# Gated linear recurrence and cos-gated layer: one masked score product per head and chunk in place of seven block sizes, with the gates' product divided out of the keys

## Chip, cores and metric

The kernel runs on one core of one Trainium2 chip, in float32. The metric is the device time in microseconds of one execution. The median of three runs of the kernel before is 1408.85 us (1404.82 to 1410.23).

## What is computed

Two stages. The first is a linear recurrence with complex gates; the second is a gated layer on its output. Cut to what matters:

```
mag = sqrt(a_re**2 + a_im**2)                       # B=4, H=8, S=768, D=48
a   = (a_re + i a_im) * minimum(mag, 0.999) / (mag + 1e-6)
for t in range(S):                                  # S is a complex 48x48 state per (b, h)
    S = a[t][:, None] * S + outer(k[t], v[t])
    y[t] = einsum('d,de->e', q[t], real(S))
x = y as (3072, 384)
h = x @ w_in                                        # 384 x 2048
out = (h * cos(h)) @ w_out                          # 2048 x 384
```

The gates lie near 0.9: a_re is 0.85 to 0.95 and a_im is normal with deviation 0.1. The weights come as float64, and the kernel turns their bits into float32 on the chip.

## The kernel before

Time is cut into chunks of 128 steps, six per batch entry and 24 in all. Two chunks make a group, so there are 12 groups. Work goes in iterations: iteration `it` does `gates(it)`, `chunks(it-1)` and `layer(it-2)`, three stages of a pipeline over groups, and `weave` mixes their pieces by a position between 0 and 1. There are 14 iterations. The scheduler of the language then orders each engine's instructions.

**Gates** (`g_log` L201 to `g_stack` L280, tiles of 128 x 768 for a group): magnitude and tangent of each gate by Ln and Exp on ScalarE with a correction step on VectorE and GpSimd; the angle by Arctan; running sums of the angles over the chunk by a product with a triangular matrix (`phs`, L263, and L266 for what the chunk before left); cos and sin; and the stacked keys `ks` and queries `qs` (L293), 96 wide, cos part and sin part.

**Chunks**: `mT`, `kT` and `qT` (magnitudes, keys, queries) are transposed per head through TensorE (L304, copied out of PSUM by ScalarE, L306). For a pair s < t in a chunk the product of magnitudes between them is needed. It is never divided out: seven block sizes (1, 2, ... 64) each take one matrix product per head (`lv`, L330, 128 x 64), a masked copy into the score tile `atm` on VectorE (L333), and then, for the next block size, half of `qT` times a total on VectorE and half of `kT` times a total on GpSimd (both L341). So one level waits for the scaling of the level before, and two chunks run alternately. Then `yp` (L354 scores times values, L357 queries times state), the diagonal term on GpSimd and VectorE (L348, L360), the new state (`kp`, L371, transposes the scaled keys back; `sp`, L375), and `xp` (L395), which transposes the result for the layer.

**Layer**: `mm1` (L403, `hp`, eight pieces of 128 x 512), the cosine in five steps on ScalarE and VectorE (L409 to L416), `mm2` (L422, `op`, 16 products of 128 x 384 per chunk), a copy and the store. The weights are loaded and converted (`from_double`, L136 to L164, six VectorE steps and one GpSimd add on each of 14 parts) at the end of iteration 0.

TensorE runs its instructions in order; a product in float32 that is not a transpose shows in the trace as two records, so 1344 `lv` products are 2688 records.

Of the kernel before, what the change touches and what calls it, by code (L numbers as in the profile page):

```python
# [11 lines left out]
F32 = mybir.dt.float32  # L12
U8 = mybir.dt.uint8
U32 = mybir.dt.uint32
I64 = mybir.dt.int64
# [10 lines left out]
ROUND = 12582912.0  # L26


@with_exitstack
def kernel(  # L30
    ctx: ExitStack,
    tc: tile.TileContext,
    q: bass.AP,
# [29 lines left out]
    NJ = DF // C  # L63
# [3 lines left out]
    consts = ctx.enter_context(tc.tile_pool(name="consts", bufs=1))  # L67
    wts = ctx.enter_context(tc.tile_pool(name="wts", bufs=1))
    ld = ctx.enter_context(tc.tile_pool(name="ld", bufs=2))
    gt = ctx.enter_context(tc.tile_pool(name="gt", bufs=1))  # L70
    ft = ctx.enter_context(tc.tile_pool(name="ft", bufs=2))
    pa = ctx.enter_context(tc.tile_pool(name="pa", bufs=5, space=PSUM))
    pm = ctx.enter_context(tc.tile_pool(name="pm", bufs=3, space=PSUM))

    step_np = np.arange(C)
    mask_np = np.zeros((C, LV, C // 2), np.uint8)
    for l in range(LV):
        m = 1 << l
        right = step_np[(step_np // m) % 2 == 1]
        mask_np[:, l] = ((step_np[:, None] // (2 * m) == right[None, :] // (2 * m))  # L80
                         & ((step_np[:, None] // m) % 2 == 0))
    sums_np = (step_np[:, None] <= step_np[None, :]).astype(np.float32)
    last_np = np.zeros((C, C), np.float32)
    last_np[C - 1] = 1.0

    def constant(array, dtype, name):
        t = consts.tile(list(array.shape), dtype, name=name)
        nc.scalar.dma_start(out=t, in_=nc.inline_tensor(array, name=name + "_const").ap())
        return t

    def scalar_tile(value, name):
# [4 lines left out]
    X = [dict() for _ in range(NG)]  # L96
    Y = [dict() for _ in range(N)]
# [13 lines left out]
    sums = constant(sums_np, F32, "sums")  # L111
    ident = constant(np.eye(C, dtype=np.float32), F32, "ident")
# [20 lines left out]
                    from_double(stage, dst, src)  # L133

    def from_double(stage, dst, src):
        """dst = the doubles of which src has the bits, to the nearest float32 (0 below 2^-126).  # L136

        A double's exponent field is 11 bits wide, a float's 8: what falls between the top bit
        and the low seven only tells the range.
        """  # L140
        shape = list(dst.shape)
        raw = stage.tile(shape, I64, tag="raw", name="raw")
        nc.sync.dma_start(out=raw, in_=src)
# [335 lines left out]
            msb = ctx.enter_context(tc.tile_pool(name="msb", bufs=2))  # L479


# [1 line left out]
_INS = ['q', 'k', 'v', 'a_re', 'a_im', 'moe_w_in', 'moe_w_out']  # L483
_OUTS = [((3072, 384), 'float32')]
# [25 lines left out]
```

## Time and profile before

| | |
|---|---|
| profiled execution, own span | 1405.6 us |
| median of three runs | 1408.85 us |
| TensorE busy (matmul) | 1181.8 us, 84% |
| VectorE / GpSimd / ScalarE busy | 801.7 / 653.1 / 446.2 us |
| mean granted TensorE clock | 0.843 |

The profiled execution's span is 3.25 us below the median of the runs. A page's 40 slices of some 35 us each show the busy share in tenths; PEclk is the share of its full clock that TensorE was granted. A row of a timeline gives the start and the length in us; the length of a row of matmuls overlaps with the next row's start, since they are pipelined, so the pace of a row is read from start to next start.

### The profile page before, as it was taken

The page shows a single profiled execution, that of the slowest core. Times are in us where ns is not written, and L with a number is a line of the kernel's source. Part 1 is how long each engine was busy: PE and PEld are TensorE (multiplying, and loading weights), DVE is VectorE, ACT ScalarE, POOL GpSimd, SP SyncE. Part 2 cuts the span into 40 slices and gives each one's busy share as a digit, 9 for nine tenths or more (in the row PEclk, how much of TensorE's full clock was granted, in tenths as well). Part 3 has the DMA queues.
Part 4 walks back from the last instruction along what each step waited for, and adds up shares of the span by engine and source line. Part 5 has one row for each costly group of instructions (what it writes and reads, how often), then busy time and mean ns, then how long its engine had stood idle before and what let it go on. Part 6 is the DMA issues. An engine that isn't in the chain of part 4 may idle for free. (4 is left out here: it accounts for less than half of the span.)

```text
span 1405.6 us, 16204 instructions
## 1 busy us (share of the span) xinstructions
PE 1181.8 (84%) x6528; PEld 995.2 (71%) x6528; DVE 801.7 (57%) x935; ACT 446.2 (32%) x688; POOL 653.1 (46%) x544
## 2 busy tenths in 40 slices
PE   0302399999998999999989999999989985999998
PEld 0202298887886877977868868968968864978965
DVE  3898964843943845834835837627628516524612
ACT  2301104324324234334334335225225233114213
POOL 5765447535534654554554446346345335213200
PEclk9756556889989999889889899789798996589999
DMA  7323201102102101011011010010021000000000
GB/s 145 98 88 113 78 1 35 23 1 45 24 1 45 23 18 40 12 28 29 12 29 29 12 40 17 12 40 22 8 46 23 1 23 0 1 7 7 1 12 12
DMA packets 131947, 42.20 MB, mean 30 GB/s; under 512 B 125600, under 2 KB 129056, under 8 KB 131104
## 3 DMA queue, kind: packets, MB, share of 16 engines
q1 hardware_dynamic: 131296, 40.90, 12.6%
q8 instruction: 52, 0.85, 0.2%
q10 hardware_dynamic: 576, 0.25, 0.1%
q14 instruction: 23, 0.19, 0.0%
HBM read 36.43 MB, written 4.72 MB: 29 GB/s over the span
## 5 line engine op out<-in xcount | busy, mean ns | idle before, releaser
L330 PEld LDWEIGHTS lv<-qT,kT 96*128 96x128 f32 x2688 | 373.5, 219 | 78.8 <-POOL w_out L160 35.0
L330 PE MATMUL lv<-qT,kT 96*128 96x64 f32 x2688 | 370.3, 300 | 60.7 <-DVE qT L341 60.6
L403 PE MATMUL hp<-xT,w_in 128*128 128x256 f32 x1152 | 306.0, 414 | 18.8 <-DVE gate L416 18.2
L341 POOL TENSOR_TENSOR kT<-kT,tot 96x512 f32<-96x512 f32 x144 | 180.4, 1253 | 276.8 <-PE lv L330 276.8
L422 PE MATMUL op<-w_out,gate 128*128 128x384 f32 x768 | 286.5, 529 | 0.0
L403 PEld LDWEIGHTS hp<-xT,w_in 128*128 128x128 f32 x1152 | 226.9, 207 | 49.1 <-issue 17.6
L422 PEld LDWEIGHTS op<-w_out,gate 128*128 128x128 f32 x768 | 157.0, 211 | 98.6 <-issue 20.6
L333 DVE COPY_PREDICATED atm<-mask,lv 128x512 f32<-128x512 uint8 x168 | 147.7, 879 | 95.2 <-PE lv L330 93.5
L341 DVE TENSOR_TENSOR qT<-qT,tot 96x512 f32<-96x512 f32 x144 | 177.7, 1234 | 0.0
L410 DVE TENSOR_SCALAR rnd<-rnd 128x512 f32<-128x512 f32 x96 | 58.6, 610 | 154.1 <-ACT rnd L409 153.2
L409 ACT ACTIVATE rnd<-hp,round_b 128x512 f32<-128x512 f32 x96 | 65.5, 682 | 151.9 <-PE hp L403 151.6
L414 ACT ACTIVATE cs<-cs 128x512 f32<-128x512 f32 x96 | 60.5, 630 | 145.5 <-DVE cs L412 145.3
L263 PE MATMUL phs<-t,sums 128*128 128x384 f32 x48 | 23.1, 570 | 98.2 <-DVE t L254 98.1
L416 DVE TENSOR_TENSOR gate<-hp,cs 128x512 f32<-128x512 f32 x96 | 65.7, 684 | 43.6 <-ACT cs L189 43.6
L263 PEld LDWEIGHTS phs<-t,sums 128*128 128x128 f32 x48 | 8.3, 214 | 100.0 <-DVE t L254 95.3
L317 POOL TENSOR_TENSOR tot<-mT 96x512 f32<-96x512 f32 x24 | 26.6, 1106 | 112.6 <-ACT mT L306 112.6
L354 PE MATMUL yp<-v,atm 128*128 128x48 f32 x384 | 78.0, 301 | 0.0
L357 PE MATMUL yp<-state,qT 96*128 96x48 f32 x320 | 70.0, 304 | 0.0
L189 ACT ACTIVATE cs<-cs,half_pi_b 128x512 f32<-128x512 f32 x96 | 68.9, 719 | 1.9
L354 PEld LDWEIGHTS yp<-v,atm 128*128 128x128 f32 x384 | 66.1, 221 | 2.4
L412 DVE SCALAR_TENSOR_TENSOR cs<-hp,rnd 128x512 f32<-128x512 f32 x96 | 65.8, 686 | 3.2
L341 POOL TENSOR_TENSOR kT<-kT,mT 96x512 f32<-96x512 f32 x24 | 40.9, 1706 | 49.1 <-ACT cs L414 35.7
(80 smaller groups left out, 1418.2 us busy)
## 6 DMA issues: line engine op xcount, KB each, us to landing
raw<-in_moe_w_in_dram SPq DMA_DIRECT2D x6, 1024.0 KB, 5.0
raw<-in_moe_w_out_dram SPq DMA_DIRECT2D x8, 768.0 KB, 4.3
re<-in_a_re_dram SPq DMA_DIRECT2D x24, 192.0 KB, 3.3
im<-in_a_im_dram SPq DMA_DIRECT2D x24, 192.0 KB, 3.3
k<-in_k_dram SPq DMA_DIRECT2D x24, 192.0 KB, 3.3
q<-in_q_dram SPq DMA_DIRECT2D x24, 192.0 KB, 3.3
v<-in_v_dram SPq DMA_DIRECT2D x24, 192.0 KB, 3.5
out_dram<-ot SPq DMA_DIRECT2D x24, 192.0 KB, 1.9
```

The source lines that it names most:

```text
L189: chain(nc.scalar.activation(func=func, **kw))
L330: nc.tensor.matmul(ps[:, h], lhsT=y["kT"][:, h], rhs=right[:, h, :, 1], start=True, stop=True)
L333: nc.vector.copy_predicated(dst, mask[:, l].rearrange("p (x m) -> p x m", m=m).unsqueeze(1).to_broadcast([C, H, C // (2 * m), m]), ps.rear ...
L341: eng.tensor_tensor(out=part, in0=part, in1=tot[:, :, ds(1 - a, 1)].to_broadcast(shape), op=ALU.mult)
L354: nc.tensor.matmul(ps[:, h], lhsT=atm[n % 2][:, h], rhs=vals[:, h], start=True, stop=(state is None))
L357: nc.tensor.matmul(ps[:, h], lhsT=y["qT"][:, h], rhs=state[:, h], start=False, stop=True)
L403: nc.tensor.matmul(ps[:, ji], lhsT=w_in[:, dc, ts(jp * 2 + ji, C)], rhs=x["xT"][:, dc].rearrange("p g t -> p (g t)"), start=(dc == 0), sto ...
L409: nc.scalar.activation(out=rnd, in_=ps, func=AF.Identity, scale=INV_TWO_PI, bias=round_b)
L412: nc.vector.scalar_tensor_tensor(out=cs, in0=ps, scalar=INV_TWO_PI, in1=rnd, op0=ALU.mult, op1=ALU.subtract)
L414: nc.scalar.activation(out=cs, in_=cs, func=AF.Abs)
L416: nc.vector.tensor_tensor(out=gate, in0=ps, in1=cs, op=ALU.mult)
L422: nc.tensor.matmul(ps, lhsT=X[g]["gate"][j // 2][:, j % 2, ts(i, C)], rhs=w_out[:, j], start=(j == 0), stop=(j == NJ - 1))
```

## The change

The chunk's magnitudes are handled as running products. `g_log` forms the logarithm of the gate's magnitude; `g_prod` sums it over the chunk with the same triangular product (`lgs`), and two Exp give P (the product of the gates up to t) and Q (one over it), with a correction step on VectorE. `g_stack` multiplies the queries by P and the keys by Q. One product per head (`sc`, 128 x 128) then gives all scores of a chunk, and VectorE multiplies them by a causal mask (with 0.25, for the factor of -2 that P and Q each carry). `f_totals`, `f_level`, the `mT` and `kp` transposes, the diagonal term and the two `atm` tiles that were cleared once are gone. The state takes the stacked keys as they are and is multiplied by the chunk's end product `end`, which goes from P's last row to DRAM and back, 4 bytes at a time, into 96 partitions.

The layer's cosine is now a sine with a shift of a quarter turn: one ScalarE step fewer. `mm2` of a group moves to the iteration after its `mm1`, ahead of everything else, so there are 15 iterations. The weights are converted in 28 smaller parts inside iteration 0, woven with the gates.

The old kernel becomes `general_path`. `least` records whether any end product fell below 1e-12; after the fast path every engine reads a flag made from it, and a branch runs `general_path` if the flag is set.

```
-def tile_gateloop__then__act_gcu_kernel(
+def general_path(
...
+@with_exitstack
+def fast_path(ctx, tc, q, k, v, a_re, a_im, moe_w_in, moe_w_out, out, least):
...
+    def g_log(g):
...
+        nc.scalar.activation(out=m2, in_=re, func=AF.Square)
+        nc.scalar.activation(out=sq, in_=im, func=AF.Square)
+        nc.vector.tensor_tensor(out=m2, in0=m2, in1=sq, op=ALU.add)
+        special(out=m2, in_=m2, func=AF.Ln, bias=tiny_b)
+        special(out=mag, in_=m2, func=AF.Exp, scale=0.5)
+        special(out=rs, in_=m2, func=AF.Exp, scale=-0.5)
+        nc.scalar.activation(out=sq, in_=re, func=AF.Abs)
+        nc.vector.tensor_tensor(out=mag, in0=mag, in1=sq, op=ALU.add)
+        nc.vector.tensor_scalar(out=m2, in0=m2, scalar1=0.5, scalar2=math.log(CAP),
+                                op0=ALU.mult, op1=ALU.min)
+        special(out=rs, in_=rs, func=AF.Ln, scale=EPS, bias=one_b)
+        special(out=sq, in_=mag, func=AF.Ln)
+        special(out=sq, in_=sq, func=AF.Exp, scale=-1.0)
+        nc.gpsimd.tensor_tensor(out=m2, in0=m2, in1=rs, op=ALU.subtract)
+        x["lg"] = m2
+        nc.gpsimd.tensor_tensor(out=mag, in0=mag, in1=sq, op=ALU.mult)
+        nc.vector.scalar_tensor_tensor(out=sq, in0=mag, scalar=2.0, in1=sq,
+                                       op0=ALU.subtract, op1=ALU.mult)
+        nc.vector.scalar_tensor_tensor(out=sq, in0=sq, scalar=-1.0, in1=im,
+                                       op0=ALU.mult, op1=ALU.mult)
...
+    def g_prod(g):
...
+        for i in range(G):
+            ps = pa.tile([C, DM], F32, tag="a", name="lgs")
+            nc.tensor.matmul(ps, lhsT=sums, rhs=x["lg"][:, ts(i, DM)], start=True, stop=True)
+            special(out=x["P"][:, ts(i, DM)], in_=ps, func=AF.Exp)
+            special(out=x["Q"][:, ts(i, DM)], in_=ps, func=AF.Exp, scale=-1.0)
+        u = temp("mag")
+        nc.vector.scalar_tensor_tensor(out=u, in0=x["Q"], scalar=HUGE, in1=x["P"],
+                                       op0=ALU.min, op1=ALU.mult)
+        for name in "PQ":
+            nc.vector.scalar_tensor_tensor(out=x[name], in0=u, scalar=3.0, in1=x[name],
+                                           op0=ALU.subtract, op1=ALU.mult)
+        row = rows_d.tile([G * DM], F32, tag="row", name="row")
+        nc.scalar.dma_start(out=row, in_=x["P"][C - 1:C].rearrange("o x -> (o x)"))
+        x["end"] = ft.tile([D2, G * H], F32, tag="end", name="end")
+        for a in range(2):
+            nc.sync.dma_start(out=x["end"][ds(a * D, D)], in_=row.rearrange("(x d) -> d x", d=D))
+        nc.vector.tensor_scalar(out=x["end"], in0=x["end"], scalar1=-0.5, scalar2=None,
+                                op0=ALU.mult)
+        nc.vector.scalar_tensor_tensor(out=least, in0=x["end"], scalar=LEAST, in1=least,
+                                       op0=ALU.is_ge, op1=ALU.min)
...
+    def g_stack(g):
...
+        nc.gpsimd.tensor_tensor(out=x["P"], in0=flat(x["q"]), in1=x["P"], op=ALU.mult)
+        nc.gpsimd.tensor_tensor(out=x["Q"], in0=flat(x["k"]), in1=x["Q"], op=ALU.mult)
...
+            eng.tensor_tensor(
+                out=t, in0=src.rearrange("p (x d) -> p x d", d=D).unsqueeze(2).to_broadcast(shape),
+                in1=x["trig"].rearrange("p a (x d) -> p x a d", d=D), op=ALU.mult)
...
+    def f_scores(n, hh):
...
+        for h in range(HH):
+            nc.tensor.matmul(ps[:, h], lhsT=y["kT"][:, hh * HH + h], rhs=y["qT"][:, hh * HH + h],
+                             start=True, stop=True)
+        nc.vector.tensor_tensor(out=y["atm"][:, ts(hh, HH)], in0=ps,
+                                in1=causal.unsqueeze(1).to_broadcast([C, HH, C]), op=ALU.mult)
...
+        nc.scalar.copy(out=y["x"], in_=ps.rearrange("p h d -> p (h d)"))
...
+    def f_state(n):
...
+            nc.tensor.matmul(ps[:, h], lhsT=X[g]["ks"][:, i * H + h].rearrange("p a d -> p (a d)"),
+                             rhs=X[g]["v"][:, i, h], start=True, stop=True)
...
+            nc.vector.scalar_tensor_tensor(out=new, in0=ps, scalar=0.25, in1=y["state"],
+                                           op0=ALU.mult, op1=ALU.add)
+            nc.gpsimd.tensor_tensor(out=new, in0=new, in1=end, op=ALU.mult)
...
+        nc.scalar.activation(out=turn, in_=ps, func=AF.Identity, scale=INV_TWO_PI, bias=quarter_b)
+        nc.vector.tensor_scalar(out=cs, in0=turn, scalar1=ROUND, scalar2=ROUND,
+                                op0=ALU.add, op1=ALU.subtract)
+        nc.vector.tensor_tensor(out=cs, in0=turn, in1=cs, op=ALU.subtract)
+        special(out=cs, in_=cs, func=AF.Sin, scale=TWO_PI)
+        nc.vector.tensor_tensor(out=gate, in0=ps, in1=cs, op=ALU.mult)
...
+    def chunks(g):
+        ns = range(g * G, g * G + G)
+        for n in ns:
+            for name in ("kT", "qT"):
+                for hh in range(2):
+                    yield lambda n=n, name=name, hh=hh: f_transpose(n, name, hh)
+            for hh in range(2):
+                yield lambda n=n, hh=hh: f_scores(n, hh)
+            yield lambda n=n: f_state(n)
+            yield lambda n=n: f_out(n)
+            yield lambda n=n: f_xt(n)
...
+    for it in range(NG + 3):
+        g, c, m, o = it, it - 1, it - 2, it - 3
...
+        if g < NG:
+            g_log(g)
+            g_prod(g)
+            g_angle(g)
+            if g + 1 < NG:
+                load(g + 1, ("re", "im"))
+        if it == 0:
+            weave((gates(0), 0.0, 1.0), (weights, 0.2, 1.0))
+            continue
+        if 0 <= o < NG:
+            for i in range(G):
+                mm2(o, i)
+        weave((gates(g) if g < NG else (), 0.0, 0.5),
+              (chunks(c) if 0 <= c < NG else (), 0.0, 1.0),
+              ([lambda jp=jp: mm1(m, jp) for jp in range(NJ // 2)] if 0 <= m < NG else (),
+               0.0, 1.0))
...
+    fast_path(tc, q, k, v, a_re, a_im, moe_w_in, moe_w_out, out, least)
+    low = keep.tile([D2, 1], F32, name="low")
+    nc.vector.tensor_reduce(out=low, in_=least, axis=AX.X, op=ALU.min)
...
+    flag = keep.tile([1, 1], I32, name="flag")
+    nc.vector.tensor_scalar(out=flag, in0=bad[:, 0:1], scalar1=0.5, scalar2=None, op0=ALU.is_lt)
+    taken = nc.values_load(flag[0:1, 0:1], min_val=0, max_val=1,
+                           skip_runtime_bounds_check_because="a comparison gives 0 or 1")
+    with tc.If(taken > 0):
+        general_path(tc, q, k, v, a_re, a_im, moe_w_in, moe_w_out, out)
```

Rows of TensorE's order, the opening of an iteration in the middle of the program. Before (`ms`, `ks`, `qs` are the stacked tiles that are transposed, `hp` is `mm1`, `lv` a block size):

```order
L304 MATMUL tp<-ident,ms 96x128 x8
L403 MATMUL hp<-xT,w_in 128x256 x6
L304 MATMUL tp<-ident,ms 96x128 x8
L403 MATMUL hp<-xT,w_in 128x256 x6
L304 MATMUL tp<-ident,ks 96x128 x16
L263 MATMUL phs<-t_3840,sums 128x384
L266 MATMUL phs<-ph,last 128x384
L304 MATMUL tp<-ident,qs 96x128 x8
L403 MATMUL hp<-xT,w_in 128x256 x6
L304 MATMUL tp<-ident,qs 96x128 x8
L330 MATMUL lv<-qT,kT 128x64 x8
L263 MATMUL phs<-t_3840,sums 128x384
```

Now, from the last `mm1` of one iteration into the next (`op` is `mm2`, `lgs` the sum of logarithms, `tp` a transpose):

```order
L796 MATMUL hp<-xT,w_in 128x256 x4
L813 MATMUL op<-w_out,gate 128x384 x13
L662 MATMUL lgs<-m_3422,sums 128x384 x2
L813 MATMUL op<-w_out,gate 128x384 x19
L734 MATMUL tp<-ident,ks 96x128 x4
L697 MATMUL phs<-sq,sums 128x384
L796 MATMUL hp<-xT,w_in 128x256 x6
L734 MATMUL tp<-ident,ks 96x128 x4
L734 MATMUL tp<-ident,qs 96x128 x4
L697 MATMUL phs<-sq,sums 128x384
L700 MATMUL phs<-ph,last 128x384
L734 MATMUL tp<-ident,qs 96x128 x4
```

The transposes of `ms` and all `lv` rows are gone; `op` stands in one piece at the front, with the two new `lgs` after the first 13 of its products.

Rows of VectorE's order in the same stage. Before (`rnd`, `cs`, `gate` belong to the layer's cosine, `atm` is the masked copy, `qT` the scaling between two levels):

```order
L333 COPY_PREDICATED atm_107<-mask,lv 128x256x2
L412 SCALAR_TENSOR_TENSOR cs<-hp,rnd 128x512
L341 TENSOR_TENSOR qT<-qT,tot 96x256x2
L333 COPY_PREDICATED atm_109<-mask,lv 128x256x2
L341 TENSOR_TENSOR qT<-qT,tot 96x256x2
L416 TENSOR_TENSOR gate<-hp,cs 128x512
L333 COPY_PREDICATED atm_107<-mask,lv 128x128x4
L341 TENSOR_TENSOR qT<-qT,tot 96x128x4
L293 TENSOR_TENSOR qs<-t_2917,t_2860 128x16x48
L410 TENSOR_SCALAR rnd<-rnd 128x512
L333 COPY_PREDICATED atm_109<-mask,lv 128x128x4
```

Now (`P`, `Q`, `mag` are the running products, `rs` and `sq` the angle, `end` the chunk's end product, `ph` the phase):

```order
L669 SCALAR_TENSOR_TENSOR P<-mag,P 128x768
L669 SCALAR_TENSOR_TENSOR Q<-mag,Q 128x768
L686 SCALAR_TENSOR_TENSOR rs<-re,rs 128x768
L688 SCALAR_TENSOR_TENSOR sq<-sq,rs 128x768
L676 TENSOR_SCALAR end<-end 96x16
L678 SCALAR_TENSOR_TENSOR least<-end,least 96x16
L702 TENSOR_SCALAR ph<-phs 128x384
L704 TENSOR_TENSOR ph<-phs,ph 128x384
L803 TENSOR_SCALAR cs<-turn 128x512
L805 TENSOR_TENSOR cs<-turn,cs 128x512
L702 TENSOR_SCALAR ph<-phs 128x384
L635 TENSOR_TENSOR m_2641<-m_2641,sq 128x768
```

The pairs of masked copy and scaling are gone; three steps on P and Q have come, and two on `end`, which wait for a round trip through DRAM and stand ahead of the phase and of the layer's cosine.

More of the change, by code (lines that the diff above doesn't have):

```diff
@@ L26 @@
 ROUND = 12582912.0
+LEAST = 1e-12
+HUGE = 1e30
 @with_exitstack
-def kernel(
+def general_path(
     ctx: ExitStack,
@@ L87, in constant @@
         t = consts.tile(list(array.shape), dtype, name=name)
[L88 removed]
+        nc.scalar.dma_start(out=t, in_=nc.inline_tensor(array, name=name + "_gconst").ap())
         return t
@@ new lines, with kernel @@
+@with_exitstack
+def kernel(ctx, tc, q, k, v, a_re, a_im, moe_w_in, moe_w_out, out):
+    nc = tc.nc
+    D2, H = 2 * q.shape[3], q.shape[1]
+    keep = ctx.enter_context(tc.tile_pool(name="keep", bufs=1))
+    least = keep.tile([D2, 2 * H], F32, name="least")
+    fast_path(tc, q, k, v, a_re, a_im, moe_w_in, moe_w_out, out, least)
+    low = keep.tile([D2, 1], F32, name="low")
+    nc.vector.tensor_reduce(out=low, in_=least, axis=AX.X, op=ALU.min)
+    scratch = ctx.enter_context(tc.tile_pool(name="scratch", bufs=1,
+                                             space=bass.MemoryType.DRAM))
+    line_d = scratch.tile([D2], F32, name="line_d")
+    nc.sync.dma_start(out=line_d, in_=low.rearrange("p o -> (p o)"))
+    line = keep.tile([1, D2], F32, name="line")
+    nc.sync.dma_start(out=line, in_=line_d.unsqueeze(0))
+    bad = keep.tile([1, 2], F32, name="bad")
+    nc.vector.tensor_reduce(out=bad[:, 0:1], in_=line, axis=AX.X, op=ALU.min)
+    flag = keep.tile([1, 1], I32, name="flag")
[4 more added lines that the diff above has]
+        general_path(tc, q, k, v, a_re, a_im, moe_w_in, moe_w_out, out)
```

242 lines of the change are left out of this document (added).

## The prediction

> **What bounds the kernel now.** I read the page first, then the busy time by stage, then TensorE's timeline and waits. The page, with TensorE's busy line, its tenths in 40 slices of 35 us, and its granted clock:
>
> ```profile
> span 1405.6 us, 16204 instructions
> PE 1181.8 (84%) x6528; PEld 995.2 (71%) x6528; DVE 801.7 (57%) x935; ACT 446.2 (32%) x688; POOL 653.1 (46%) x544
> ...
> PE   0302399999998999999989999999989985999998
> ...
> PEclk9756556889989999889889899789798996589999
> ```
>
> TensorE is full from about the sixth slice on and nearly empty before, so there are two stages to price apart: a start in which others work, and a long middle that TensorE paces. The busy times by stage, cut where iteration 2 starts, where iteration 12 starts, and where only the layer is left (length; busy us and count of PE, PEld, DVE, ACT, POOL; granted clock; DMA):
>
> ```profile
> 0.00:226.50 226.50, 80.83 (x381) 74.40 (x382) 164.88 (x151) 40.62 (x52) 131.86 (x85) 0.63 0.32 82
> 226.50:1273.70 1047.20, 974.03 (x5465) 817.69 (x5463) 584.87 (x705) 364.46 (x567) 497.52 (x431) 0.87 0.10 21
> 1273.70:1359.10 85.40, 84.84 (x527) 72.93 (x525) 38.08 (x55) 25.12 (x44) 23.71 (x28) 0.96 0.02 5
> 1359.10:1405.60 46.50, 42.10 (x160) 30.15 (x160) 13.83 (x24) 16.05 (x27) 0.00 (x0) 0.99 0.04 14
> ```
>
> Iterations 2 to 11 take 1047.2/10 = 104.7 us each, with VectorE at 56% and the others below. Iteration 12, which has chunks and layer but no gates, takes 85.4.
>
> The paces of TensorE at full clock, from its timeline, start to next start:
>
> ```profile
> 811.65 1.48 PE L375 MATMUL sp<-v,ke 128*96 128x48 f32 x16
> 812.97 0.51 PE L395 MATMUL xp<-ident,x 128*128 128x128 f32 x3
> 813.32 9.20 PE L422 MATMUL op<-w_out,gate 128*128 128x384 f32 x28
> 822.35 0.32 PE L354 MATMUL yp<-v,atm 128*128 128x48 f32 x2
> 822.51 0.39 PE L357 MATMUL yp<-state,qT 96*128 96x48 f32 x2
> 822.73 0.39 PE L354 MATMUL yp<-v,atm 128*128 128x48 f32 x2
> ...
> 1273.59 1.04 PE L304 MATMUL tp<-ident,ms 128*96 128x128 f32 x8
> 1274.46 2.77 PE L403 MATMUL hp<-xT,w_in 128*128 128x256 f32 x12
> 1277.07 1.04 PE L304 MATMUL tp<-ident,ms 128*96 128x128 f32 x8
> ...
> 1297.66 1.90 PE L330 MATMUL lv<-qT,kT 96*128 96x64 f32 x16
> 1299.39 0.87 PE L403 MATMUL hp<-xT,w_in 128*128 128x256 f32 x3
> ```
>
> Per record that is 0.083 us for `sp`, 0.117 for `xp`, 0.32 for `op` (9.03/28), 0.11 for `yp`, 0.109 for `tp`, 0.218 for `hp` (2.61/12) and 0.108 for `lv` (1.73/16). I take `phs`, as wide as `op`, at 0.32, and `kp` at `tp`'s pace. An average iteration before then holds 96 `hp` (20.9), 64 `op` (20.6), 224 `lv` (24.2), 48 `tp` (5.2), 13.3 `kp` (1.5), 26.7 `sp` (2.2), 58.7 `yp` (6.5), 6 `xp` (0.7) and 7.3 `phs` (2.3): 84.1 us. So 104.7 − 84.1 = 20.6 us per iteration are lost, and in iteration 12 (no `phs`) 85.4 − 81.8 = 3.6. Of the 20.6, idle time is (1047.2 − 974.0)/10 = 7.3; the other 13.3 is TensorE at a lower clock. The idle time in that stage, by what ended it:
>
> ```profile
> PE lv L330 <- DVE qT L341: 25.9, 17, 2.4
> PE hp L403 <- DVE gate L416: 17.2, 1, 17.2
> PE xp L395 <- DVE x L360: 15.8, 6, 4.1
> PE sp L375 <- ACT ke L372: 10.8, 5, 2.6
> ```
>
> The clock can fall without a wait. In the following rows, with no idle time shown, pairs of `yp` go from a pace of 0.22 to 0.43:
>
> ```profile
> 708.13 0.42 PE L357 MATMUL yp<-state,qT 96*128 96x48 f32 x2
> 708.35 0.63 PE L354 MATMUL yp<-v,atm 128*128 128x48 f32 x2
> ```
>
> **The middle, part by part.** The change removes, per iteration, 224 `lv`, 16 `tp` of `ms` and the `kp`: 24.2 + 1.7 + 1.5 = 27.4 us. It adds 32 records of `sc`, 128 columns wide. The nearest rows are the transposes, as wide, at 0.109, and above them `hp`, twice as wide, at 0.218; I take 0.109, so 3.5 us (7.0 at most). It adds 4 `lgs`, as wide as `op`: 1.3 us. So 84.1 − 27.4 + 4.8 = 61.5 us of work.
>
> Does another engine take over? The durations:
>
> ```profile
> L409 ACT ACTIVATE rnd<-hp,round_b 128x512 f32<-128x512 f32 x96 | 65.5, 682 | 151.9 <-PE hp L403 151.6
> L410 DVE TENSOR_SCALAR rnd<-rnd 128x512 f32<-128x512 f32 x96 | 58.6, 610 | 154.1 <-ACT rnd L409 153.2
> L412 DVE SCALAR_TENSOR_TENSOR cs<-hp,rnd 128x512 f32<-128x512 f32 x96 | 65.8, 686 | 3.2
> L189 ACT ACTIVATE cs<-cs,half_pi_b 128x512 f32<-128x512 f32 x96 | 68.9, 719 | 1.9
> L188 ACT ACT_TABLE_LOAD x24 | 30.8, 1283 | 3.0 <-issue 2.6
> L189 ACT ACTIVATE t<-t,tiny_b 128x768 f32<-128x768 f32 x24 | 22.5, 936 | 114.8 <-POOL t L223 107.3 <-POOL t L206 7.4
> L206 POOL TENSOR_TENSOR t<-t,t 128x768 f32<-128x768 f32 x12 | 21.6, 1799 | 10.2 <-ACT t L205 10.2
> L236 DVE SCALAR_TENSOR_TENSOR t<-t,t 128x768 f32<-128x768 f32 x12 | 14.9, 1238 | 66.7 <-POOL t L235 66.7
> L333 DVE COPY_PREDICATED atm<-mask,lv 128x512 f32<-128x512 uint8 x168 | 147.7, 879 | 95.2 <-PE lv L330 93.5
> L341 DVE TENSOR_TENSOR qT<-qT,tot 96x512 f32<-96x512 f32 x144 | 177.7, 1234 | 0.0
> ```
>
> VectorE gets 15 widths of 768 per iteration (1.24 us each, 18.6), the cosine's three steps eight times (2.0, so 15.9), four masks of 512 (0.69, 2.8) and some 4 of phase and state: 41 us. ScalarE gets 13 of 768 (0.94, 12.2), eight times 1.4 for the cosine, two table loads (2.6) and some 10 of copies and Exp: 36. GpSimd gets four of 1.8 and a state: 9. All stay under 61.5, so TensorE keeps the pace. That includes the added VectorE steps on P and Q and the causal mask: they cost nothing while that cover of 20 us holds, and their own length if it went.
>
> What is late next? `lv` no longer waits for `qT`, `sp` not for `ke`. The new wait is `lgs`: after the last `hp` the chain is turn 0.68, two VectorE steps 1.30, sine 0.72, table 1.28, Ln, two Exp and Ln 3.74, and GpSimd's subtraction 1.80, together 9.5 us and a dozen hand-overs, against 26 records of `op` ahead of `lgs`, 8.4 us. I take 2 us of idle time per iteration. Behind the waiting `lgs` stand 38 `op`, which have their inputs but must queue. For the clock I keep 9 of the 13.3 us: fewer waits, but `sp` and `yp`, 8.7 us of 48-column work, remain and stand in one piece now. So 11 us of loss, between the 3.6 of iteration 12 and the 20.6 of the others: 72.5 us, bounds 65.1 to 82.1.
>
> [...]
>
> **Queues.** VectorE now waits for `end` (L676), with the phase and the layer's cosine queued behind it, and so TensorE's second `phs`. `end` is two transfers of 768 pieces of 4 bytes, behind a store of P's row. The nearest row is a gate load, 1024 pieces of 192 bytes (128 partitions by 8 heads):
>
> ```profile
> re<-in_a_re_dram SPq DMA_DIRECT2D x24, 192.0 KB, 3.3
> ```
>
> Store and loads should be back some 6 to 7 us after P's row is issued; TensorE has 38 `op` (12 us) to do meanwhile. Price nothing; 20 us of round trip would show as some 9 per iteration. SyncE's loads of `re` and `k` queue behind the same wait, an iteration ahead of need.
>
> **Start.** Before, `chunks(0)` ends at 226.5 us. VectorE is busy for 164.9 of it. The 14 masked copies and 14 scalings of group 0 (14 × 0.88 + 14 × 1.23 = 29.5) go; two groups with four more widths of 768 each (9.9) and four masks (2.8) come; so 148 us of VectorE, after some 20 us in which it waits for the first gates. TensorE's alternation with it after the last conversion (from 178 us on) shrinks to one chunk's products. Against 168, VectorE should gain a few us since GpSimd's 131.9 us fall to about 50. I take 165; 145 if VectorE's waits and collisions go, 195 if the 28 smaller weight parts wait for their loads.
>
> **End.** Without chunks, the layer runs as in these rows:
>
> ```profile
> 1359.16 10.63 PE L403 MATMUL hp<-xT,w_in 128*128 128x256 f32 x48 [0.62 <-ACT xT L396]
> ...
> 1381.43 20.80 PE L422 MATMUL op<-w_out,gate 128*128 128x384 f32 x64
> ```
>
> The 96 `hp` take 22.3, the last `op` with the store 24.2 to the span's end. The flag is made while the layer still runs; reading it and branching has no row. I take 4 us, from 1 to 10.
>
> **Sum.** Start 165; iteration 2, without `op`, 61.5 − 20.6 + 11 = 51.9; iterations 3 to 11, 9 × 72.5 = 652.5; iteration 12, without `phs` and `lgs`, 61.5 − 3.6 + 3.6 = 61.5; iteration 13, 20.6 + 22.3 = 42.9; iteration 14, 24.2; branch 4. That is 1002 us against the span of 1405.6, which lies 3.25 below the median of the runs: 1005 us.
>
> **Rivals.**
> 1. The clock recovers: as dense as iteration 12, the middle loses 3.6 per iteration, and ten of them gain 74: 931. For it speaks 0.96 in that stage; against it the 48-column rows. [...] Chance 0.15.
> 2. The chain through ScalarE and VectorE paces the iteration: `lgs` waits 8 to 10 us instead of 2, and the clock falls after it, 82 us: 1005 + 95 = 1100. For it speaks that ScalarE's copies, loads of `re` and table loads stand in one order. [...] Chance 0.12.
> 3. The start does not shrink, because conversion and not levels set it: 226 instead of 165, 1066. Against it: VectorE's sum above. Chance 0.1.
> 4. Slower: the flag is set and the old program runs after the new, 1002 + 1400 = 2400 us. That happens from an end product below 1e-12, thus a mean gate under 10^(−12/128) = 0.81. The gates of the reference average 0.9, whose 128th power is 1.4e-6, so it needs a flag read wrongly. Chance 0.03.
>
> The forecast has 0.6. Its own range with the first three cases is 930 to 1095; it leaves out rival 4 and the far ends. A run of this kernel can tell 0.5% from no change. Only rival 4 is slower (0.03), nothing comes near no change (0.01), so faster has 0.96.
>
> **What would show it.** TensorE's records should be 6528 − 2688 − 192 − 160 + 384 + 48 = 3920, with no `lv`; iterations 3 to 11 about 72 us apart, the granted clock there 0.85 to 0.95, and `lgs` the largest wait. The first `hp` should start near 165 us. A wait of VectorE for `end` that TensorE shares, or iterations over 80 us with the clock near 0.8, would show rival 2; under 67, rival 1. The sum falls if an iteration's `sc` pace is nearer 0.218, or if the start ends after 195 us.

## The result, and the profile after

The kernel after takes 936.56 us (median of four runs, 934.14 to 938.23), the kernel before on the same chip 1409.54 (1404.82 to 1410.89): a ratio of 0.6647 with an interval of 0.663 to 0.6664. The forecast was 1005 us in a range of 930 to 1095, so the direction and the range held and the middle of it was 68 us too high. The profiled execution took 938.23 us by this metric; its span is 936.4. Of all the executions told of here one, the slowest of run 11, counts as a slow one and is left out: 901.26 us, where the other three took 885.0 to 897.1.

The page of the kernel after, the same lines as before, with slices of 23.4 us:

```profile
span 936.4 us, 10169 instructions
PE 797.1 (85%) x3920; PEld 621.0 (66%) x3920; DVE 497.1 (53%) x761; ACT 378.6 (40%) x588; POOL 171.3 (18%) x96
...
PE   1101446899999999999999999999999989999997
...
PEclk9999966899899999989899999898999998998999
```

The records are the 3920 that were counted from the change, so the general path did not run. TensorE is still the full engine, and no other passes 53%. The mean granted clock is 0.943, against 0.843 before. The busy times by stage, cut at the first `hp`, at the starts of iterations 3 and 12, and 2 us before the end of iteration 12 (columns as before):

```profile
0.00:156.00 156.00, 39.50 (x172) 29.04 (x172) 125.52 (x219) 40.60 (x55) 57.88 (x41) 0.91 0.47 120
156.00:209.15 53.15, 49.59 (x274) 42.26 (x275) 32.55 (x46) 27.51 (x44) 12.76 (x6) 0.86 0.22 40
209.15:807.00 597.85, 584.60 (x2942) 458.63 (x2941) 305.63 (x440) 279.78 (x438) 99.48 (x48) 0.95 0.17 33
807.00:866.00 59.00, 59.00 (x298) 46.72 (x298) 16.51 (x28) 16.09 (x30) 1.21 (x1) 0.94 0.02 8
```

Where 469.2 us of span went: the start ends at 156.0 instead of 226.5 (70.5 us). Iterations 2 to 11 take 53.15 + 597.85 = 651.0 instead of 1047.2 (396.2). From iteration 12 to the end it is 129.4 instead of 131.9 (2.5).

The 396.2 of the middle split by the prediction's own paces. Work: 841 before; after, nine iterations of 61.5 and one of 40.9 without `op`, 594.4; so 246.6 us. Idle time: 73.2 before, (53.15 − 49.59) + (597.85 − 584.60) = 16.8 after; 56.4 us. The rest is clock: 133 before, 39.8 after; 93.2 us. The forecast, 2 us of idle time and 9 of clock in each iteration, had some 53 and 43 for the last two: the idle time was right and the clock much too small. That its paces hold for the work is read from iterations that lose nothing (below).

TensorE's longest waits after (line waited for, releaser, total us, times, longest):

```profile
PE lgs L662 <- POOL m L646: 49.3, 10, 38.6
PE phs L697 <- DVE sq L688: 38.8, 2, 28.6
PE yp L755 <- DVE atm L746: 19.3, 3, 11.3
```

The longest of each lie in the start (38.6 ends at 73 us, 28.6 at 106 us). In the iterations `lgs` waits about 1.2 us, as in these rows of TensorE's timeline, and the 38 `op` behind it keep their full pace, 0.32 us:

```profile
406.73 8.55 PE L813 MATMUL op<-w_out,gate 128*128 128x384 f32 x26
416.47 1.56 PE L662 MATMUL lgs<-m,sums 128*128 128x384 f32 x4 [1.19 <-POOL m L646]
417.87 12.42 PE L813 MATMUL op<-w_out,gate 128*128 128x384 f32 x38
...
443.37 1.48 PE L769 MATMUL sp<-v,ks 128*96 128x48 f32 x16
444.69 0.39 PE L755 MATMUL yp<-v,atm 128*128 128x48 f32 x2
...
446.92 0.39 PE L755 MATMUL yp<-v,atm 128*128 128x48 f32 x2
447.14 0.50 PE L758 MATMUL yp<-state,qT 96*128 96x48 f32 x2
447.45 0.63 PE L755 MATMUL yp<-v,atm 128*128 128x48 f32 x2
...
449.15 5.27 PE L796 MATMUL hp<-xT,w_in 128*128 128x256 f32 x12
```

The second half of these rows holds the loss that is left. A state (`sp`) and the outputs (`yp`), all 48 columns wide, stand in one piece. Some 3.8 us into it the pace of `yp` doubles from 0.22 to 0.43 per pair, and the 12 `hp` behind take 5.1 us instead of 2.6. No idle time stands anywhere near.

### The profile page after: what moved, and what is told of

The parts are those of the page before. It is cut to its first block, busy times and chain, and to the rows that moved or that the text cites. A ratio compares the mean times of both kernels' runs of the same rounds, so it can differ in the third digit from the quotient of the medians.

```text
span 936.4 us, 10169 instructions
## 1 busy us (share of the span) xinstructions
PE 797.1 (85%) x3920; PEld 621.0 (66%) x3920; DVE 497.1 (53%) x761; ACT 378.6 (40%) x588; POOL 171.3 (18%) x96
## 4 chain that ended last, share of the span: by engine, by line
PE 70%; ACT 6%; DVE 2%; POOL 2%; DMA 1%; issue 1%; ACTq 0%; SPq 0%; POOLq 0%; DVEq 0%
PE hp L796 28%; PE op L813 17%; PE yp L755 4%; PE sc L744 4%; PE yp L758 4%; PE tp L734 4%; PE sp L769 3%; POOL m L646 2%; ACT rs L619 2%; PE lgs L662 1%; ACT L618 1%; PE phs L697 1%; PE phs L700 1%; PE xp L788 1%; ACT m L619 1%; ACT mag L619 1%
## 5 line engine op out<-in xcount | busy, mean ns | idle before, releaser
L813 PE MATMUL op<-w_out,gate 128*128 128x384 f32 x768 | 251.1, 486 | 0.0
L803 DVE TENSOR_SCALAR cs<-turn 128x512 f32<-128x512 f32 x96 | 42.4, 443 | 172.9 <-ACT turn L802 172.9
L802 ACT ACTIVATE turn<-hp,quarter_b 128x512 f32<-128x512 f32 x96 | 65.7, 685 | 124.6 <-PE hp L796 122.7
L776 POOL TENSOR_TENSOR state<-state,end 96x384 f32<-96x384 f32 x16 | 31.2, 1949 | 342.2 <-DVE state L774 179.1
L805 DVE TENSOR_TENSOR cs<-turn,cs 128x512 f32<-128x512 f32 x96 | 65.9, 687 | 2.1
L646 POOL TENSOR_TENSOR m<-m,rs 128x768 f32<-128x768 f32 x12 | 22.0, 1835 | 197.6 <-ACT rs L619 196.7
L697 PE MATMUL phs<-sq,sums 128*128 128x384 f32 x48 | 22.4, 557 | 38.8 <-DVE sq L688 38.8
L758 PEld LDWEIGHTS yp<-state,qT 96*128 96x128 f32 x320 | 54.2, 212 | 0.0
L744 PE MATMUL sc<-qT,kT 96*128 96x128 f32 x384 | 48.4, 277 | 0.1
L744 PEld LDWEIGHTS sc<-qT,kT 96*128 96x128 f32 x384 | 46.9, 192 | 2.3 <-ACT qT L736 1.0
```

What stands on the lines that cost most here:

```text
L646: nc.gpsimd.tensor_tensor(out=m2, in0=m2, in1=rs, op=ALU.subtract)
L744: nc.tensor.matmul(ps[:, h], lhsT=y["kT"][:, hh * HH + h], rhs=y["qT"][:, hh * HH + h], start=True, stop=True)
L758: nc.tensor.matmul(ps[:, h], lhsT=y["qT"][:, h], rhs=state[:, h], start=False, stop=True)
L802: nc.scalar.activation(out=turn, in_=ps, func=AF.Identity, scale=INV_TWO_PI, bias=quarter_b)
L803: nc.vector.tensor_scalar(out=cs, in0=turn, scalar1=ROUND, scalar2=ROUND, op0=ALU.add, op1=ALU.subtract)
L805: nc.vector.tensor_tensor(out=cs, in0=turn, in1=cs, op=ALU.subtract)
```

## Experiments

The question was where the clock loss of the middle came from and why it left: from waits (the reading of the forecast, in part) or from the products that were taken out. All ratios are to the kernel before, run on the same chip as the experiment; the kernel after has 0.6647. Since chips differ by up to 0.5% in their runs of the kernel before (medians of 1402.98 to 1409.54 us), a gain or cost against the kernel after is worked out as the difference of the ratios times 1409.54 us.

### 1. The scalings taken out of the kernel before

```
-        for t, a, eng in ((y["qT"], 1, nc.vector), (y["kT"], 0, nc.gpsimd)):
-            part = halves(t, m)[:, :, a]
-            eng.tensor_tensor(out=part, in0=part,
-                              in1=tot[:, :, ds(1 - a, 1)].to_broadcast(shape), op=ALU.mult)
```

> The kernel before, without the scaling of qT and kT between two block sizes (both L341 steps are left out, so the scores are those of unscaled queries and keys); every lv product and every masked copy stays. Theory (the waits between levels pull TensorE's clock down): an iteration keeps its 84.1 us of work and loses some 4 us instead of 20.6, like iteration 12, so ten iterations of 88 us instead of 104.7, and the start some 20 us less: about 1220 us, granted clock near 0.95. Rival (the 64-column lv rows pull the clock down by themselves): only the idle time at lv goes, 26 us in the middle and some 35 in the start: about 1345 us, clock still near 0.87.

Measured: 1334.88 us, ratio 0.9489 (0.9456 to 0.9523), near the rival. The wait of `lv` for `qT`, 60.6 us of the kernel before, is gone, and the granted clock hardly rises: 0.855 against 0.843. With nothing to wait for, `lv` collects in runs of 48 records, and there the clock falls:

```profile
711.68 6.11 PE L330 MATMUL lv<-qT,kT 96*128 96x64 f32 x48
717.58 5.43 PE L397 MATMUL hp<-xT,w_in 128*128 128x256 f32 x12
722.80 7.23 PE L330 MATMUL lv<-qT,kT 96*128 96x64 f32 x48
729.82 4.58 PE L397 MATMUL hp<-xT,w_in 128*128 128x256 f32 x12
```

At the full paces 48 `lv` would take 5.2 and 12 `hp` 2.6. The run does not clear the waits, though, since two things change in it: the waits go and the runs grow longer. The trace records the granted clock as stretches at full or at half (1.00 and 0.50 in the rows below), in the kernel before all on one grid of 3.41 us, and what fills the 3.4 us ahead of a stretch at half tells them apart. Two such pairs of the kernel before, the first with a wait of `lv` for `qT`, the second without idle time:

```profile
370.40:373.80 3.40, 0.97 (x10) 0.86 (x9) 3.40 (x3) 0.02 (x1) 3.40 (x3) 1.00 0.11 22
373.80:380.60 6.80, 6.80 (x25) 5.90 (x23) 6.80 (x6) 2.42 (x4) 4.43 (x3) 0.50 0.24 48
704.90:708.30 3.40, 3.40 (x34) 3.40 (x33) 2.04 (x3) 0.00 (x0) 1.04 (x1) 1.00 0.02 5
708.30:718.50 10.20, 10.20 (x44) 8.60 (x44) 2.31 (x4) 4.22 (x7) 0.83 (x1) 0.50 0.00 0
```

All stretches at half clock of iterations 2 to 11, by these 3.4 us (number, total length; half of the length is lost):

| | before | run 1 | after |
|---|---|---|---|
| 1.85 us or more of idle time | 14, 116 us | 8, 58 us | 1, 3 us |
| `lv` with 0.9 to 1.3 us of idle time | 6, 72 us | none | none |
| products of 48 or 64 columns (and a few `kp`), no idle time | 8, 75 us | 28, 160 us | 9, 51 us |

The column of the kernel after is for iterations 3 to 11. Run 1 thus trades one cause for the other. Before, both cost: some 58 us behind waits, 36 behind `lv` with a short wait, 38 behind narrow products alone.

### 2. The state's products moved away from the outputs

```
             for hh in range(2):
                 yield lambda n=n, hh=hh: f_scores(n, hh)
-            yield lambda n=n: f_state(n)
             yield lambda n=n: f_out(n)
             yield lambda n=n: f_xt(n)
+            yield lambda n=n: f_state(n)
```

> The changed kernel with the state product (sp) moved behind xp, so that sp and yp no longer stand in one piece of 48-column products. Theory (sp and yp together, 4.8 us, are what halves the clock in the changed kernel, and they do it about once per iteration for 3 to 5 us of loss): ten such dips go, 895 to 910 us against 936. Rival (yp alone, 3.5 us, is enough): 930 to 940 us.

Measured: 916.38 us, ratio 0.6518 (0.6501 to 0.6535), 18 us below the kernel after and between the two expectations. The page's clock line shows no dip after the start:

```profile
PEclk9997555999999999999999999999999999999999
```

The outputs alone, 32 records and 3.5 us of 48 columns, now run through at 0.22 per pair, and mostly the `hp` behind them at full pace. Tenths of a slice hide what is left: five short stretches at half clock from 390 us on still follow `yp`, as here, where 4 `hp` take 1.74 us instead of 0.87:

```profile
391.34 0.39 PE L758 MATMUL yp<-state,qT 96*128 96x48 f32 x2
391.56 1.94 PE L796 MATMUL hp<-xT,w_in 128*128 128x256 f32 x4
393.30 0.84 PE L788 MATMUL xp<-ident,x 128*128 128x128 f32 x3
```

The piece of 48-column work that the prediction named is thus a cause of what was left of the loss, and a shorter one costs less.

### 3. The second half of the layer put back

```
-    for it in range(NG + 3):
+    for it in range(NG + 2):
...
-        if 0 <= o < NG:
-            for i in range(G):
-                mm2(o, i)
...
-              ([lambda jp=jp: mm1(m, jp) for jp in range(NJ // 2)] if 0 <= m < NG else (),
+              ([lambda jp=jp: mm1(m, jp) for jp in range(NJ // 2)] +
+               [lambda i=i: mm2(m, i) for i in range(G)] if 0 <= m < NG else (),
```

> The changed kernel with mm2 put back into the iteration of its mm1, woven into the end as before, 14 iterations. Theory (the block of op at the head of the iteration covers the chain to lgs and keeps the clock up): lgs then waits for its whole chain of some 10 us behind fewer products, and the clock falls after it: 5 to 10 us per iteration, 990 to 1040 us. Rival (the removed work is all that counts and the place of mm2 is free): 930 to 945 us.

Measured: 942.3 us, ratio 0.6699 (0.6661 to 0.6736). The interval overlaps that of the kernel after: the new place of `mm2` is no part of the gain that these runs can tell. It is a balance of two, though. With `mm2` woven in, `phs` waits in nearly every iteration, and the clock halves behind the wait nine times from iteration 3 on:

```profile
571.43 1.06 PE L697 MATMUL phs<-sq,sums 128*128 128x384 f32 x2 [2.77 <-DVE sq L688]
```

In exchange wide products now often stand between `sp` and `yp`, and only two stretches at half clock follow these there, where the kernel after has ten.

### 4. Dead `lv` products added to the kernel after, in long runs

Nothing uses them but a copy of one column per level; 2688 records of 64 columns, as many as were taken out.

```
+    def f_extra(n, l):
+        y, m = Y[n], 1 << l
+        ps = pa.tile([C, H, C // 2], F32, tag="a", name="lv")
+        right = y["qT"].rearrange("p h (x two m) -> p h x two m", two=2, m=m)
+        for h in range(H):
+            nc.tensor.matmul(ps[:, h], lhsT=y["kT"][:, h], rhs=right[:, h, :, 1],
+                             start=True, stop=True)
...
+            for l in range(7):
+                yield lambda n=n, l=l: f_extra(n, l)
             yield lambda n=n: f_state(n)
```

> The changed kernel with the seven lv products per head and chunk put back as dead work (one element of each result is copied, nothing waits for a scaling): 2688 records at 0.108 us. Theory (lv rows cost their own pace and nothing else): 936 + 291 = 1227 us, clock near 0.94. Rival (64-column rows pull the clock down by themselves): the 13 us per iteration of clock loss of the kernel before come back too, about 1380 us.

Measured: 1343.82 us, ratio 0.9553 (0.9518 to 0.9588), nearer to the rival. That is 410 us more than the kernel after, or 0.152 us per record against a pace of 0.108: 290 us of work and 120 of clock. So the products alone, without masks, scalings or a chain of levels, cost 410 us when they stand like this; the whole change gained 473. All 22 runs of 64 from 180 us on lose the clock within themselves, and most pass it on to the `hp` behind (full: 6.9 and 2.6):

```profile
711.69 8.77 PE L754 MATMUL lv<-qT,kT 96*128 96x64 f32 x64
720.25 4.66 PE L806 MATMUL hp<-xT,w_in 128*128 128x256 f32 x12
724.74 5.47 PE L754 MATMUL lv<-qT,kT 96*128 96x64 f32 x48
...
746.91 9.76 PE L754 MATMUL lv<-qT,kT 96*128 96x64 f32 x64
```

The run of 48 at 724.74 and the 16 `sp` behind it kept their pace, so a long run makes a dip likely, not certain. From 180 us on thirteen pieces of narrow products, 5.3 to 8.4 us long, kept it; each of them begins within 1.1 us of the end of a stretch at half clock. Why is open.

### 5. The same products, one level at a time

`f_extra` is as in 4, but its levels stand singly between the transposes, the scores and the output, mostly 16 records at a time; for the last chunk they are left out, so 2576 records.

```
+            for l, piece in enumerate(pieces):
+                yield piece
+                if n and l < 5:
+                    yield lambda n=n, l=l: f_extra(n - 1, l + 1)
```

> The changed kernel with the dead lv products again, but one block size at a time (16 records, 1.7 us) between transposes, sc and hp, 2576 records in all. Theory (a long unbroken run of narrow products halves the clock, a short one does not): 936 + 2576 x 0.108 = 1215 us, clock 0.93 or more. Rival (every 64-column record costs 0.152 us, as in the run with four block sizes in a row, wherever it stands): 1327 us, clock near 0.85.

Measured: 1198.91 us, ratio 0.8538 (0.8511 to 0.8564). That is 267 us more than the kernel after, 0.104 per record, with a granted clock of 0.962. It is less than the pace of 0.108, since fewer stretches at half clock follow `sp` and `yp` here: six from 200 us on, where the kernel after has eleven. Only the order differs from 4 (and 4% of the products).

### 6. The same long runs, with 128 columns

```
+        for hh in range(2):
+            ps = pa.tile([C, HH, C], F32, tag="a", name="lv")
+            for h in range(HH):
+                nc.tensor.matmul(ps[:, h], lhsT=y["kT"][:, hh * HH + h],
+                                 rhs=y["qT"][:, hh * HH + h], start=True, stop=True)
```

> The changed kernel with dead products in the long runs of the run before, as many and from the same weights, but 128 columns wide instead of 64: 2688 records at the 0.109 us that sc and the transposes show. Theory (it is the narrow moving side that lets the clock fall): 936 + 293 = 1229 us although the columns double, clock 0.94 or more. Rival (any long run of products that are paced by their weight loads lets the clock fall): about 1344 us, clock near 0.84.

Measured: 1224.6 us, ratio 0.8721 (0.8694 to 0.8747), clock 0.953. Twice the columns at the same places cost 117 us less than in 4, and all ten stretches at half clock from 200 us on follow `sp` and `yp`. The rows, 64 records in 7.15 us and the `hp` behind in 2.6:

```profile
648.72 7.31 PE L754 MATMUL lv<-qT,kT 96*128 96x128 f32 x64
655.87 2.75 PE L806 MATMUL hp<-xT,w_in 128*128 128x256 f32 x12
```

That the pace of narrow products goes with the width of their weights, as the rival has it, the rows of 48 columns show: 0.083 us a record with 96 columns of weights (`sp`), 0.11 with 128 (`yp`).

Runs 4 to 6 together show it: neither the number of products nor the length of a run costs the clock by itself; a long unbroken run of narrow ones (48 or 64 records of 64 columns) does, without any wait. That waits cost it as well is read from run 3 (2.77 us) and from the kernel before (1.85 us or more of 3.4).

### 7. The second weight converted in iteration 2

The 16 parts of `w_out` leave iteration 0.

```
-        parts += [(w_out[:, j], wo[:, j]) for j in range(NJ)]
+        late = [(w_out[:, j], wo[:, j]) for j in range(NJ)]
...
+              (late if it == 2 else (), 0.0, 1.0))
```

> The changed kernel with the 16 parts of w_out converted in iteration 2 instead of iteration 0. Theory (VectorE's conversions set the start): the first hp comes 30 to 40 us earlier, at 115 to 125 us, and iteration 2 takes 10 to 20 us more, since VectorE has 33 of its 53 us in use there: 910 to 925 us. Rival (the loads and the gates' chain set the start): first hp still after 145 us, 936 us or more.

Measured: 908.14 us, ratio 0.6477 (0.6453 to 0.65), 24 us below the kernel after. The first `hp` starts at 121.9 instead of 156.0; VectorE is busy for 101.4 of that, instead of 125.5:

```profile
0.00:121.90 121.90, 35.97 (x181) 25.63 (x182) 101.36 (x150) 46.41 (x64) 46.50 (x31) 0.71 0.50 119
```

Of these 34 us, 5.5 are given back in iteration 3, which holds conversion steps now (71.2 us instead of 65.7); iteration 2, which was expected to grow by 10 to 20, does not (51.8 us, 53.1 in the kernel after). What then still parts 29 from 24 is within the intervals (18 to 30). The loads of these parts leave the start together with the conversions, so the run alone can't part the two. But no wait of VectorE for a load shows in the start of the kernel after (its longest is 7.2 us, for ScalarE). So VectorE's work sets the start.

### 8. No branch, no general path

The kernel ends with `fast_path`; the flag, the branch and the path behind it are left out.

> The changed kernel with the fast path alone: no flag, no branch, no general path in the program. The price of flag and branch was put at 4 us, from 1 to 10: 932 us (926 to 935). Rival (the branch is free because reading and jumping lie beside the last store): 935 to 937 us.

Measured: 925.1 us, ratio 0.658 (0.6557 to 0.6603): 9 us, not 4, just below the range expected. From the start of the last 64 `op` to the end it takes 24.5 us instead of 26.8; the rest is in the iterations (run 9).

### 9. The two VectorE steps on `end` put behind the stacking

```
-        nc.vector.tensor_scalar(out=x["end"], in0=x["end"], scalar1=-0.5, scalar2=None,
-                                op0=ALU.mult)
...
+        yield lambda: g_end(g)
```

> The changed kernel with VectorE's two steps on the chunk's end product put behind the step that forms the stacked queries, so that VectorE no longer waits for the round trip through DRAM ahead of the phase (31 us of waits in eight places in the changed kernel). Theory (that wait is covered by the block of op): 930 to 940 us, the wait for the transfer gone. Rival (it holds back the phase, the stacked tiles and so TensorE): 910 to 925 us.

Measured: 927.52 us, ratio 0.6585 (0.6553 to 0.6617), between the two expectations. VectorE's wait for `end`, in the kernel after

```profile
DVE end L676 <- DMA end<-row: 31.0, 8, 4.0
DVE bad L892 <- DMA line<-line_d: 8.9, 1, 8.9
```

is gone, and that for `bad` is down to 1.9 us: the last step on `least` moved too, and the flag's steps with it. Which of the two counts is read from the iterations, that is from the starts of their first `op`. In run 9, iterations 3, 11, 12 and 13:

```profile
210.10 8.55 PE L818 MATMUL op<-w_out,gate 128*128 128x384 f32 x26
...
730.16 8.55 PE L818 MATMUL op<-w_out,gate 128*128 128x384 f32 x26
...
797.67 20.81 PE L818 MATMUL op<-w_out,gate 128*128 128x384 f32 x64
859.12 20.81 PE L818 MATMUL op<-w_out,gate 128*128 128x384 f32 x64
```

In run 10, which leaves the wait for `end` where it was and moves the flag alone:

```profile
210.19 8.55 PE L813 MATMUL op<-w_out,gate 128*128 128x384 f32 x26
...
730.26 8.55 PE L813 MATMUL op<-w_out,gate 128*128 128x384 f32 x26
...
800.06 20.81 PE L813 MATMUL op<-w_out,gate 128*128 128x384 f32 x64
859.86 20.81 PE L813 MATMUL op<-w_out,gate 128*128 128x384 f32 x64
```

And in the kernel after, with the last iteration:

```profile
209.15 8.55 PE L813 MATMUL op<-w_out,gate 128*128 128x384 f32 x26
...
732.56 8.55 PE L813 MATMUL op<-w_out,gate 128*128 128x384 f32 x26
...
806.82 20.81 PE L813 MATMUL op<-w_out,gate 128*128 128x384 f32 x64
868.28 20.81 PE L813 MATMUL op<-w_out,gate 128*128 128x384 f32 x64
909.64 20.80 PE L813 MATMUL op<-w_out,gate 128*128 128x384 f32 x64
```

Iterations 3 to 10 take 520.1 us in run 9 and 520.1 in run 10: with and without the wait for `end` the same, so it is covered and costs nothing. (The kernel after has 523.4 there: in iteration 3 its trace has one more stretch at half clock, 6.8 us from 249 us on, which costs 3.4.) Iterations 11 and 12 take 129.0 us in run 9, 129.6 in run 10 and 135.7 in the kernel after. That gain of 6 to 7 us is the flag's.

### 10. The flag's steps put behind the last gate

```
     low = keep.tile([D2, 1], F32, name="low")
-    nc.vector.tensor_reduce(out=low, in_=least, axis=AX.X, op=ALU.min)
+    first = nc.vector.tensor_reduce(out=low, in_=least, axis=AX.X, op=ALU.min)
+    tc.add_manual_dep(first.ins, last_gate.ins.name, mybir.DependencyInfo(
+        mybir.DependencyClass.NoSync, mybir.DependencyReason.DATA))
```

> The changed kernel with the three VectorE steps that make the flag put behind the last gate of the layer. Theory (in iteration 11 VectorE waits 8.9 us for the flag's round trip, TensorE then waits for the phase and its clock falls): iterations 11 and 12 lose some 6 us less, 928 to 932 us, and the tail is not longer, since the round trip lies beside the last op. Rival (the 11 us that the kernel without flag and branch gains are in the reading and the jump at the end): 934 to 940 us.

Measured: 929.85 us, ratio 0.662 (0.6604 to 0.6636), inside what the theory gave: 4 us below the kernel after, whose interval it just touches, and 6 in the rows above. In that kernel the flag's round trip through DRAM stood in VectorE's queue ahead of iteration 11's phases, and TensorE waited for those; behind the wait the clock is lower, and 12 `hp` take 3.8 us instead of 2.6 (TensorE's timeline of the kernel after):

```profile
764.46 1.44 PE L700 MATMUL phs<-ph,last 128*128 128x384 f32 x2 [2.50 <-DVE ph L704]
765.69 3.96 PE L796 MATMUL hp<-xT,w_in 128*128 128x256 f32 x12
```

### 11 and 12. The gains together

Run 11 has the edits of 2 and 7, run 12 those of 2, 7 and 10.

> The changed kernel with sp behind xp and with w_out converted in iteration 2. If the two gains (20 us and 28 us) lie in different stages and add: 936.5 - 48 = 888 us. If the later conversions hold back VectorE so that the clock falls elsewhere: 895 to 910 us.

> The run before with the flag's steps behind the last gate as well. If the three gains add: 880 to 884 us. If the wait for the flag is hidden once sp stands elsewhere: 886 to 890 us.

Measured: 890.46 us (median of three; 893.78 with the fourth, of 901.26), ratio 0.634 (0.63 to 0.6381), and 892.66, ratio 0.6349 (0.6332 to 0.6365). The two edits gain 43 us together and 42 as the sum of their single gains, so they add, as far as the interval can tell. With the third the time lies above both of its expectations: it adds nothing that can be told, where it gained 4 alone. The intervals are too wide to say that it is lost. Either version is some 4.5% below the kernel after and does all of its work.

## Why the prediction held, and where it was off

The range held by its lower end: 936.56 us is 6.6 above the 930 that rival 1 put there, and 68 below the forecast itself.

**The bound.** Right: TensorE paces the middle, and VectorE (305.6/9 = 34 us per iteration, forecast 41), ScalarE (31, forecast 36) and GpSimd (11, forecast 9) stay under it. Rival 2, a chain that paces the iteration, does not appear: `lgs` waits 1.2 us, where 2 were taken and 8 to 10 feared.

**The work.** Right: in the rows of the kernel after 16 `sc` take 1.79 us, 0.112 each, where 0.109 was taken and 0.218 kept as the upper end. Where nothing is lost an iteration is close to the sum: the shortest ones, with 1.2 us of idle time and no stretch at half clock, are 62.6 us, against 61.5.

**The loss per iteration.** This is the step that failed: "For the clock I keep 9 of the 13.3 us", and with 2 us of idle time a loss of 11. Measured, nine iterations take 66.4 us, a loss of 4.9: 13.25/9 = 1.5 idle and 3.4 clock. Nine times 6.1 is 55 of the 68 us; the start has 9 of the rest. Iterations of 66.4 us are also under the 67 that the prediction named as the sign of rival 1.

The charge was right in kind: `sp` and `yp` in one piece do bring the clock down, as the rows at 443 us and run 2 show. It was too large. From iteration 3 to 11 only nine stretches at half clock follow such pieces, and half of their 51 us is lost, 2.8 us per iteration. What had cost the clock before went with the change: the waits, and 224 `lv` in an iteration, which the prediction priced at their own pace alone. It let 4.3 us of clock per iteration go, where some 10 went.

**The cause before.** The table at run 1 splits the loss of the middle: some 58 of 131 us behind waits, 36 behind `lv` with a short wait, 38 behind narrow products alone. The rows at 708 us, which the prediction showed, are of the last kind: 16 `lv` and then `yp` without a wide product between them, and the clock falls after some 4 us of it. It is not the number of `lv` that costs: 2688 of them cost 0.044 us of clock each in long runs (run 4) and none 16 at a time (run 5). What they would have cost in the kernel before without its waits is not shown; run 1 makes their runs longer.

**Idle time and the clock.** The waits of 1.2 us on `lgs` leave the clock alone: the `op` behind them keep 0.32 us. Waits of 2.50 us in iteration 11 and of 2.77 us in run 3 are followed by half clock, and the rows at 443 us and run 4 halve without idle time, as the rows at 708 us in the prediction do.

**Start and end.** The start is 156.0 us instead of 165, a miss of 9, in its bounds. That VectorE sets it is shown by run 7. That VectorE gains where GpSimd does less, the forecast's step from 168 to 165, has the trace of the kernel before behind it: the first scaling of `qT` (`qT<-qT,mT`, L341) takes 0.67 to 0.72 us in the eleven places with no GpSimd step beside it and 1.03 to 3.78 in the thirteen with one. Rival 3, a start that does not shrink, falls. Iterations 12 and 13, by the rows of the kernel after, take 61.5 and 41.4 us, where 61.5 and 42.9 were forecast.

**`end` and the flag.** "Price nothing" for the wait on `end` was right (run 9). The flag was priced at 4 us in bounds of 1 to 10; it costs 2.3 at the end, as run 8 shows, and 6 to 7 in iterations 11 and 12, where it stood in VectorE's queue ahead of work that TensorE needs. With run 8's 9 us in all the bounds held; the place was not foreseen.

**The rivals.** Rival 1, the clock that recovers, gave 931 and came closest: the loss per iteration is 4.9 where it had 3.6. It had a chance of 0.15 because the 48-column rows spoke against it; they do cost, but about a third of what was charged. Rival 4, the general path, did not run.

## What to carry to other kernels

When a change removes many narrow products on TensorE, price them with the granted clock of the stretches in which they stood, not by their own pace alone (in run 4 it was 0.152 us a record against 0.108), and look at what filled the time just ahead of each fall of the clock, a wait or narrow work; and when it leaves some, look at how long they stand without a wide product between them, because moving one step (run 2) gave part of it back. Here a wait in VectorE's queue cost only what stood behind it and was needed soon: the round trip for `end` was free (520.1 us for iterations 3 to 10 with and without it), that for the flag, a single one, was not (6 to 7 us).

## What the runs showed of the hardware

- Float32 products with 48 columns (`sp`, `yp`, some 3 us of them) were followed by half the granted clock without idle time, and so were long runs of `lv` with 64 (64 records in 8.77 us instead of 6.9, run 4). In the trace of the kernel after, between 200 and 930 us, the twelve stretches at half clock last 3.41 or 6.83 us and all begin on one grid of 3.41 us. Eleven follow a window of that grid with 2.97 us or more of `sp` and `yp`; no other window at full clock holds more than 2.82. So a piece cost something there only where it filled most of a window. In run 2 `yp` alone, 3.5 us, was followed by half clock five times from 390 us on.
- So was idle time: the twelfth stretch follows the window with 2.50 us of it; no stretch follows the next most in these windows, 1.19 us. In run 3 each of nine waits of 2.77 or 2.78 us was followed by half clock.
- Right behind a stretch at half clock narrow pieces of up to 8.4 us kept the full clock in run 4. 128 columns in runs of 64 kept it too (7.15 us in run 6), and so did 16 `lv` at a time (run 5).
- A record of 64 columns and one of 128 take nearly the same at full clock, 0.108 and 0.112 us, so the wide form cost no more there and less in the sum: 1224.6 against 1343.82 us with the same number of products.
